# The last row of wo, loaded with its 2 KB blocks dealt in eights to the partitions

## The chip, the cores and the metric

The kernel runs on one core of one Trainium2 chip. A core has five engines with instruction queues of their own: TensorE (PE; its weight loads are shown apart as PEld), VectorE (DVE), ScalarE (ACT), GpSimd (POOL) and SyncE (SP). Sixteen DMA engines move data between HBM and the on-chip memory SBUF, which has 128 partitions; matmuls write to PSUM. Engines wait for one another through semaphores. The metric is the device time of one execution in microseconds (us).

## The reference: what is computed

One token of 1024 numbers goes through a layer norm, giving `xn`. Two branches use it, and both are added to the token:

```python
x = A_x
xn = _layernorm(x, axis=-1)
return x + _A_ref(xn, A_k_cache, A_v_cache, A_wq, A_wo) + _B_ref(xn, B_w1, B_b1, B_w2, B_b2)
```

Branch A is attention for one query position with 32 query heads and 4 key/value heads of size 128, over the last 4096 positions of the cache:

```python
q = (x @ wq).reshape(B, Sq, Hq, Dh).transpose(0, 2, 1, 3)
scores = jnp.einsum("bhqd,bhkd->bhqk", q, k) * (Dh ** -0.5)
p = _softmax(scores, axis=-1)
o = jnp.einsum("bhqk,bhkd->bhqd", p, v)
return o.transpose(0, 2, 1, 3).reshape(B, Sq, Hq * Dh) @ wo
```

Branch B is a small network: a second layer norm, `w1` (1024 x 3584) with bias `b1`, a gelu, `w2` (3584 x 1024) with bias `b2`. All inputs are bf16. The weights and the part of the caches that is used come to nearly 40 MB, and every byte of it is used once.

## The kernel before

**Loads.** All large loads are issued by SP, in this order: k (four loads, L73), wq (two, L90), w1 (two, L206), v (three, L212), w2 (two, L220) and wo (six, L228). They go into a ring of four tiles of 32 KB per partition (`ring_tile`), so a load is issued when the tile that it overwrites has been used. The DMA engines work through them in the order of issue. The small inputs (x, b1, b2) are loaded through ACT's queue (L75 to L81).

**wo.** `wo` is 4096 x 1024. `wo_v` (L222) views it as 128 partitions x 32 rows x 1024: partition p holds the rows 32p to 32p + 31 of the matrix. In what follows "row c of wo" is the slice `wo_v[:, c, :]`, that is one block of 1024 numbers (2 KB) for each of 128 partitions. Rows 0 to 15 come with one load into tile `wo0`. Rows 16 to 31 go into tile `wo1` in five loads, cut at 0, 8, 12, 14, 15 and 16 (L223), so that the last loads are small: rows 24 to 27, 28 and 29, 30, and 31.

**Compute up to the attention output.** The layer norms (L126 to L170) run on DVE, PE and POOL; POOL computes the power in L145 and L168 (`rstd`). DVE transposes k in blocks (L185), and ACT and DVE move the blocks into place (L199, L201). PE computes q (L237), the w1 products (L257), the scores (L275), and after the softmax the attention output `o_all` (L319). DVE makes `o_bf` of it (L322 to L326), which has a query head in each of 32 partitions and 128 numbers along the row.

**o8.** The product with wo needs o spread over 128 partitions in the same order as wo's rows: partition p, column c must hold number 32p + c of o. Number 32p + c belongs to head p // 4, at place 32 (p % 4) + c. Four matmuls (L328, L329) do that with the matrix `spread` (L111 to L114), made by POOL from a memset and a select: `spread[h, q, p]` is 1 where p = 4h + q and 0 elsewhere. DVE copies the result from PSUM to `o8` (L331).

**The last products.** `chunk_src` lists 28 rows of w2 ("h") and 32 rows of wo ("o"). The first 52 are the bulk (L336 to L339): two matmuls of 512 columns for each, added up in `accf`. The last eight (`TAIL`), rows 24 to 31 of wo, use four matmuls of 256 columns each (L351 to L354) into `acct`. While their loads arrive, DVE and ACT copy `accf` to `bulk` (L348, L350). At the end DVE adds `acct` and `bulk` (L356) and SP stores the result (L357).

Within an engine the order is that in which the instructions were emitted, except where the tile framework moved an instruction that has no dependence on its neighbours: on POOL the select for `spread` (L113) runs after the first `rstd` (L145), and the memset of `bulk` (L343) before it.

Of the kernel before, what the change touches and what calls it, by code (L numbers as in the profile page):

```python
# [9 lines left out]
BF16 = mybir.dt.bfloat16  # L10
# [6 lines left out]
def kernel(  # L17
# [14 lines left out]
    nc = tc.nc  # L32
    P = 128
# [5 lines left out]
    Hq = NQ // Dh  # L39
# [8 lines left out]
    CWO = NQ // P  # L48
# [6 lines left out]
    consts = ctx.enter_context(tc.tile_pool(name="consts", bufs=1))  # L55
# [8 lines left out]
    def ring_tile(name):  # L64
        return ring.tile([P, RING_ELEMS], BF16, tag="ring", name=name, align_bytes=256)
# [21 lines left out]
    for i in range(2):  # L87
        t = ring_tile(f"wq{i}")
        tv = t[:].rearrange("p (r n) -> p r n", r=4)
# [21 lines left out]
    spread = consts.tile([Hq, 4, P], BF16)  # L111
    nc.gpsimd.memset(spread[:], 0.0)
    nc.gpsimd.affine_select(out=spread[:], in_=spread[:], compare_op=ALU.not_equal, fill=1.0, base=0,  # L113
                            pattern=[[-1, 4], [1, P]], channel_multiplier=-4)  # L114

    gmask = consts.tile([Hq, Hkv], FP32)
    nc.gpsimd.memset(gmask[:], 1.0)
# [57 lines left out]
    for half in range(2):  # L175
        pr = 32 * half
        nc.tensor.matmul(accf[pr:pr + 1, :], lhsT=ones_bf[pr:pr + 2, 0:1], rhs=xb2[pr:pr + 2, :],
                         start=True, stop=False, tile_position=(pr, pr))
# [24 lines left out]
    for i in range(2):  # L203
        t = ring_tile(f"w1{i}")
        tv = t[:, :4 * Fd].rearrange("p (r n) -> p r n", r=4)
# [10 lines left out]
    for i in range(2):  # L216
        nr = CW2 // 2
        t = ring_tile(f"w2{i}")
        tv = t[:, :nr * D].rearrange("p (r n) -> p r n", r=nr)
        nc.sync.dma_start(out=tv, in_=w2_v[:, nr * i:nr * (i + 1), :])  # L220
        chunk_src += [("h", nr * i + r, tv[:, r, :]) for r in range(nr)]
    wo_v = A_wo.rearrange("(p c) n -> p c n", p=P)  # L222
    for i, cuts in enumerate([[0, 16], [0, 8, 12, 14, 15, 16]]):  # L223
        nr = CWO // 2
        t = ring_tile(f"wo{i}")
        tv = t[:].rearrange("p (r n) -> p r n", r=nr)
        for a, b in zip(cuts[:-1], cuts[1:]):
            nc.sync.dma_start(out=tv[:, a:b, :], in_=wo_v[:, nr * i + a:nr * i + b, :])  # L228
        chunk_src += [("o", nr * i + r, tv[:, r, :]) for r in range(nr)]


    for i, w3 in enumerate(wq_tiles):
        for r in range(4):
            c = 4 * i + r
            for j in range(NJQ):
                b, t = divmod(j, 4)
                nc.tensor.matmul(accq[32 * t:32 * t + 1, b, :], lhsT=xnT[:, c:c + 1], rhs=w3[:, r, j * 512:(j + 1) * 512],  # L237
                                 start=(c == 0), stop=(c == C - 1), tile_position=(0, 32 * t))
# [8 lines left out]
    for j in range(8):  # L247
        t, b = divmod(j, 2)
        nc.tensor.matmul(acch[32 * t:32 * t + 1, b, :NH], lhsT=ones_bf[0:1, 0:1], rhs=b1_row[:, j * NH:(j + 1) * NH],
                         start=True, stop=False, tile_position=(0, 32 * t))  # L250
    for i, w3 in enumerate(w1_tiles):
        for r in range(4):
            c = 4 * i + r
            for b in range(2):
                for t in range(4):
                    j = 2 * t + b
                    nc.tensor.matmul(acch[32 * t:32 * t + 1, b, :NH], lhsT=yT[:, c:c + 1], rhs=w3[:, r, j * NH:(j + 1) * NH],  # L257
                                     start=False, stop=(c == C - 1), tile_position=(0, 32 * t))
# [3 lines left out]
    for g in range(Hkv):  # L262
        b, th = divmod(g, 2)
# [6 lines left out]
    for a in range(WQ4 // 512):  # L270
        sp = ps_f.tile([P, 512], FP32, tag="pf", name="sp")
        for R in range(4):
            for g in range(Hkv):
                c0 = WQ4 * R + 512 * a
                nc.tensor.matmul(sp[32 * R:32 * R + 32, :], lhsT=qm[:, g, :], rhs=kT[:, g, c0:c0 + 512],  # L275
                                 start=(g == 0), stop=(g == Hkv - 1), tile_position=(0, 32 * R))
# [41 lines left out]
    for c in range(NCH):  # L318
        nc.tensor.matmul(o_all[:].rearrange("h g d -> h (g d)"), lhsT=eTb[:, 32 * c:32 * c + 32], rhs=v4[:, :, c, :],  # L319
                         start=(c == 0), stop=(c == NCH - 1))  # L320
# [4 lines left out]
    o_bf = consts.tile([Hq, Dh], BF16)  # L325
    nc.vector.tensor_copy(out=o_bf[:], in_=o_f[:])  # L326
    o8_ps = ps_f.tile([P, 32], FP32, tag="pf", name="o8_ps")
    for q in range(4):  # L328
        nc.tensor.matmul(o8_ps[:], lhsT=spread[:, q, :], rhs=o_bf[:, 32 * q:32 * q + 32], start=(q == 0), stop=(q == 3))  # L329
    o8 = consts.tile([P, 32], BF16)  # L330
    nc.vector.tensor_copy(out=o8[:], in_=o8_ps[:])  # L331

# [3 lines left out]
    for idx, (kind, c, wap) in enumerate(chunk_src[:n_bulk]):  # L336
        for half in range(2):
            nc.tensor.matmul(accf[32 * half:32 * half + 1, :], lhsT=vec[kind](c), rhs=wap[:, half * 512:(half + 1) * 512],  # L338
                             start=False, stop=(idx == n_bulk - 1), tile_position=(0, 32 * half))  # L339
# [11 lines left out]
    for idx, (kind, c, wap) in enumerate(chunk_src[n_bulk:]):  # L351
        for t in range(4):
            nc.tensor.matmul(acct[32 * t:32 * t + 1, :], lhsT=vec[kind](c), rhs=wap[:, t * 256:(t + 1) * 256],
                             start=(idx == 0), stop=(idx == TAIL - 1), tile_position=(0, 32 * t))  # L354
# [33 lines left out]
```

## Time and profile before

| what | value |
|---|---|
| time, median of 3 runs | 102.38 us (102.35 to 102.53) |
| profiled execution, first to last instruction (span) | 100.7 us; a time of its own beside the span is not listed |
| PE / DVE / ACT / POOL busy | 49% / 49% / 34% / 4% of the span |
| moved by DMA | 39.92 MB in 3031 packets, mean 396 GB/s |
| last load of wo | issued at 73.20 us, landed at 97.32 us |
| copy of o8 from PSUM (L331) | starts at 73.72 us, 0.19 us |
| PE waits for the first rows of wo (L338) | 6.09 us, until 87.59 us |
| L353, groups of the tail | 94.88, 96.10, 96.73 and 97.36 us |

Times in the profile count from the first instruction. A line such as `97.36 0.31 PE acct L353 x4` in the chain gives the start, the duration, the engine, the tile that is written, the line of the kernel and how many instructions were merged. "DMA wo<-in_A_wo_dram" in the chain is the time from the issue of a load to its landing, waiting behind other loads included. A table by stretches has one line for each stretch A:B, with its length, the busy time and number of instructions of PE, PEld, DVE, ACT and POOL, the granted clock of TensorE (1.00 is full), the mean busy share of the sixteen DMA engines, and the rate in GB/s. In the rows over 40 slices each digit is a share in tenths.

### The profile page before, as it was taken

What the parts mean: (1) busy time and instruction counts of PE and PEld (TensorE: products, weight loads), DVE (VectorE), ACT (ScalarE), POOL (GpSimd) and SP (SyncE); (2) the same over time, 40 slices, a digit from 0 to 9 for tenths busy, and PEclk for the clock granted to TensorE, in tenths of its full rate; (3) what the DMA queues carried; (4) which work ended last, traced back from release to release, by engine and by line L of the source; (5) the groups of instructions that cost most, each with busy time, mean ns of one, the idle gap of its engine ahead of it and who ended that gap; (6) DMA issues with size and microseconds to landing.
All of it is one profiled execution on the core that took longest, in us unless ns stands there. A gap on an engine that the chain in (4) does not pass through costs nothing.

```text
span 100.7 us, 962 instructions
## 1 busy us (share of the span) xinstructions
PE 49.1 (49%) x361; PEld 19.2 (19%) x361; DVE 49.4 (49%) x91; ACT 34.2 (34%) x37; POOL 4.5 (4%) x18
## 2 busy tenths in 40 slices
PE   0027200008500930482882935999389930299830
PEld 0012200003100300121531222334133410023310
DVE  4335499999999999997126115510630000000130
ACT  0500002999999999962001045400000000000110
POOL 7105300000000000000000000000000000000000
PEclk9999999999985579555555555569976997559995
DMA  3899999999999998999999998999999998999910
GB/s 52 346 434 436 482 443 482 443 430 417 417 417 391 456 444 376 459 444 382 391 423 430 436 511 387 467 428 433 433 410 413 456 456 384 423 420 408 369 33 1
DMA packets 3031, 39.92 MB, mean 396 GB/s; under 512 B 458, under 2 KB 466, under 8 KB 851
## 3 DMA queue, kind: packets, MB, share of 16 engines
q1 hardware_dynamic: 2872, 39.85, 93.3%
q8 instruction: 3, 0.05, 0.2%
q10 hardware_dynamic: 154, 0.01, 0.1%
q14 instruction: 2, 0.01, 0.0%
HBM read 39.86 MB, written 0.00 MB: 396 GB/s over the span
## 4 chain that ended last, share of the span: by engine, by line
DVE 37%; DMA 24%; PE 19%; issue 9%; POOL 3%; ACT 2%; SPq 2%; POOLq 1%; DVEq 0%; ACTq 0%
DMA wo<-in_A_wo_dram 24%; DVE kt_scr L185 17%; DVE kT L201 16%; PE o_all L319 10%; PE sp L275 4%; PE acch L257 3%; SPq L228 2%; ACT e L297 1%; DVE eTb L299 1%; DVE m_loc L283 1%; PE qT_ps L261 1%; DVE q_sb L240 1%; POOLq L383 1%; ACT sc L280 1%; POOL spread L113 1%
## 5 line engine op out<-in xcount | busy, mean ns | idle before, releaser
L199 ACT COPY kT<-kt_scr 32x1024 bf16<-32x1024 bf16 x26 | 27.1, 1042 | 12.9 <-DVE kt_scr L185 12.6
L185 DVE STREAM_TRANSPOSE kt_scr<-k_sb 128x4096 bf16<-128x4096 bf16 x4 | 17.4, 4412 | 0.0
L201 DVE COPY kT<-kt_scr 32x1024 bf16<-32x1024 bf16 x38 | 15.9, 419 | 0.5
L237 PE MATMUL accq<-wq,xnT 128*1 128x512 bf16 x64 | 7.1, 622 | 17.9 <-DMA wq<-in_A_wq_dram 17.9
L350 ACT COPY bulk<-accf 1x256 f32<-1x256 f32 x2 | 0.7, 361 | 31.7 <-DVE bulk L348 31.7
L348 DVE COPY bulk<-accf 1x256 f32<-1x256 f32 x2 | 0.8, 416 | 21.3 <-PE accf L338 20.8
L319 PE MATMUL o_all<-v_sb,eTb 128*32 128x512 bf16 x32 | 9.9, 485 | 1.0 <-DVE zcol L310 1.0
L338 PE MATMUL accf<-wo,o 128*1 128x512 bf16 x48 | 7.1, 465 | 6.1 <-DMA wo<-in_A_wo_dram 6.1
L257 PE MATMUL acch<-w,yT 128*1 128x448 bf16 x64 | 6.3, 574 | 5.6 <-DMA w<-in_B_w_dram 5.6
L338 PE MATMUL accf<-w,hT 128*1 128x512 bf16 x56 | 7.9, 452 | 0.0
L237 PEld LDWEIGHTS <-xnT 128*1 128x1 bf16 x64 | 2.1, 115 | 22.1 <-issue 22.1
L319 PEld LDWEIGHTS <-eTb 128*32 128x32 bf16 x32 | 3.7, 119 | 6.8 <-issue 3.8
L338 PEld LDWEIGHTS <-o 128*1 128x1 bf16 x48 | 2.4, 98 | 10.8 <-issue 8.9
L275 PE MATMUL sp<-kT,qm 128*32 128x512 bf16 x32 | 3.8, 629 | 0.3 <-DVE qm L266 0.3
L257 PEld LDWEIGHTS <-yT 128*1 128x1 bf16 x64 | 2.0, 116 | 9.4 <-issue 9.4
L131 PE MATMUL ln_tot<-st,ones_f 128*128 128x1 f32 x2 | 0.6, 362 | 6.4 <-DVE st L129 6.4
L338 PEld LDWEIGHTS <-hT 128*1 128x1 bf16 x56 | 2.7, 96 | 4.7 <-issue 2.3
L322 DVE TENSOR_TENSOR o_m<-o_all,grs 32x512 f32<-32x512 f32 x1 | 0.7, 679 | 5.6 <-PE o_all L319 5.6
L297 ACT ACTIVATE e<-sc,nmx 128x1024 bf16<-128x1024 f32 x1 | 1.1, 1147 | 5.7 <-DVE nmx L294 5.7
L314 DVE STREAM_TRANSPOSE hT<-h_sb 128x896 bf16<-128x896 bf16 x1 | 1.7, 1711 | 2.4 <-ACT h_sb L312 2.4
L261 PE MATMUL qT_ps<-ident,q_sb 128*128 128x128 bf16 x8 | 1.2, 308 | 2.3 <-DVE q_sb L240 2.3
L275 PEld LDWEIGHTS <-qm 128*32 128x32 bf16 x32 | 2.1, 133 | 1.4 <-issue 0.9
(84 smaller groups left out, 34.4 us busy)
## 6 DMA issues: line engine op xcount, KB each, us to landing
w<-in_B_w_dram SPq DMA_DIRECT2D x4, 3584.0 KB, 26.1
wq<-in_A_wq_dram SPq DMA_DIRECT2D x2, 4096.0 KB, 21.6
k_sb<-in_A_k_cache_dram SPq DMA_DIRECT2D x4, 1024.0 KB, 7.1
wo<-in_A_wo_dram SPq DMA_DIRECT2D x1, 4096.0 KB, 29.4
v_sb<-in_A_v_cache_dram SPq DMA_DIRECT2D x1, 2048.0 KB
v_sb<-in_A_v_cache_dram SPq DMA_DIRECT2D x2, 1024.0 KB, 23.4
wo<-in_A_wo_dram SPq DMA_DIRECT2D x1, 2048.0 KB
wo<-in_A_wo_dram SPq DMA_DIRECT2D x1, 1024.0 KB, 23.1
```

The costliest lines, as they stand in the source:

```text
L185: nc.vector.transpose(out=scr[:, g, :], in_=k2[:, g, :])
L199: nc.scalar.copy(out=dst, in_=src)
L201: nc.vector.tensor_copy(out=dst, in_=src)
L228: nc.sync.dma_start(out=tv[:, a:b, :], in_=wo_v[:, nr * i + a:nr * i + b, :])
L237: nc.tensor.matmul(accq[32 * t:32 * t + 1, b, :], lhsT=xnT[:, c:c + 1], rhs=w3[:, r, j * 512:(j + 1) * 512], start=(c == 0), stop=(c == C ...
L257: nc.tensor.matmul(acch[32 * t:32 * t + 1, b, :NH], lhsT=yT[:, c:c + 1], rhs=w3[:, r, j * NH:(j + 1) * NH], start=False, stop=(c == C - 1) ...
L261: nc.tensor.transpose(qT_ps[:, b * 4 + hh, :], q_sb[:, b, hh * Dh:(hh + 1) * Dh], ident[:])
L275: nc.tensor.matmul(sp[32 * R:32 * R + 32, :], lhsT=qm[:, g, :], rhs=kT[:, g, c0:c0 + 512], start=(g == 0), stop=(g == Hkv - 1), tile_posit ...
L297: nc.scalar.activation(out=e128[:], in_=sc[:], func=ACT.Exp, bias=nmx[:], scale=scale, accum_out=l_loc[:])
L314: nc.vector.transpose(out=hT[:], in_=h_sb[:].rearrange("p (d c) -> p c d", c=CW2))
L319: nc.tensor.matmul(o_all[:].rearrange("h g d -> h (g d)"), lhsT=eTb[:, 32 * c:32 * c + 32], rhs=v4[:, :, c, :], start=(c == 0), stop=(c == ...
L338: nc.tensor.matmul(accf[32 * half:32 * half + 1, :], lhsT=vec[kind](c), rhs=wap[:, half * 512:(half + 1) * 512], start=False, stop=(idx == ...
```

## The change

Row 31 of wo is loaded in another arrangement. Its 128 blocks of 2 KB are the matrix rows 32p' + 31 for p' = 0 to 127. Before, block p' goes to partition p'. After, p' is written as 8b + a with a from 0 to 7 and b from 0 to 15, and the source is walked with a outermost: block 8b + a goes to partition 16a + b. The access pattern of the source then has the sizes 8, 16 and 1024, and that of the destination 128 and 1024. The row is still one load, issued last of all on SP's queue, of the same 256 KB.

Column 31 of `o8` has to stand in the same order. A second matrix `spread_p` is made from `spread` by a copy on POOL that permutes its 128 columns in the same way (32 partitions x 512, bf16). The four matmuls of L329 now make the columns 0 to 30, and four more, of one column each, make column 31 with `spread_p`. The copy to `o8` and everything behind it stay as they were.

```diff
@@ -112,6 +112,8 @@
     nc.gpsimd.memset(spread[:], 0.0)
     nc.gpsimd.affine_select(out=spread[:], in_=spread[:], compare_op=ALU.not_equal, fill=1.0, base=0,
                             pattern=[[-1, 4], [1, P]], channel_multiplier=-4)
+    spread_p = consts.tile([Hq, 4, P], BF16)
+    nc.gpsimd.tensor_copy(out=spread_p[:].rearrange("h q (a b) -> h q a b", a=8), in_=spread[:].rearrange("h q (b a) -> h q a b", a=8))
 
@@ -220,12 +222,14 @@
     wo_v = A_wo.rearrange("(p c) n -> p c n", p=P)
-    for i, cuts in enumerate([[0, 16], [0, 8, 12, 14, 15, 16]]):
+    for i, cuts in enumerate([[0, 16], [0, 8, 12, 14, 15]]):
         nr = CWO // 2
         t = ring_tile(f"wo{i}")
         tv = t[:].rearrange("p (r n) -> p r n", r=nr)
         for a, b in zip(cuts[:-1], cuts[1:]):
             nc.sync.dma_start(out=tv[:, a:b, :], in_=wo_v[:, nr * i + a:nr * i + b, :])
+        if i == 1:
+            nc.sync.dma_start(out=tv[:, nr - 1, :], in_=wo_v[:, CWO - 1, :].rearrange("(b a) n -> a b n", a=8))
         chunk_src += [("o", nr * i + r, tv[:, r, :]) for r in range(nr)]
@@ -326,7 +330,9 @@
     o8_ps = ps_f.tile([P, 32], FP32, tag="pf", name="o8_ps")
     for q in range(4):
-        nc.tensor.matmul(o8_ps[:], lhsT=spread[:, q, :], rhs=o_bf[:, 32 * q:32 * q + 32], start=(q == 0), stop=(q == 3))
+        nc.tensor.matmul(o8_ps[:, 0:31], lhsT=spread[:, q, :], rhs=o_bf[:, 32 * q:32 * q + 31], start=(q == 0), stop=(q == 3))
+    for q in range(4):
+        nc.tensor.matmul(o8_ps[:, 31:32], lhsT=spread_p[:, q, :], rhs=o_bf[:, 32 * q + 31:32 * q + 32], start=(q == 0), stop=(q == 3))
     o8 = consts.tile([P, 32], BF16)
```

## The prediction

> **What bounds the kernel now.** I read the busy table and the queue table first, then the chain that ended last, then the busy time of short stretches at the end.
>
> From the page: the queue table, and the slices of DMA share and rate.
>
> ```profile
> DMA  3899999999999998999999998999999998999910
> GB/s 52 346 434 436 482 443 482 443 430 417 417 417 391 456 444 376 459 444 382 391 423 430 436 511 387 467 428 433 433 410 413 456 456 384 423 420 408 369 33 1
> ...
> q1 hardware_dynamic: 2872, 39.85, 93.3%
> q8 instruction: 3, 0.05, 0.2%
> ```
>
> No compute engine is over half busy (PE and DVE 49%), while the sixteen DMA engines are busy from slice 2 to slice 38 and SP's queue fills 93.3% of their time. The kernel is one stream of 39.85 MB, and its time is that stream, its start (first data at 1.8 us) and what follows its last packet. The three instruction packets (q8, 16 KB each) will matter.
>
> The end of the chain, asked for from 70 us:
>
> ```profile
> 73.20 24.12 DMA wo<-in_A_wo_dram
> 97.32 0.04 issue
> 97.36 0.31 PE acct L353 x4
> 97.67 0.03 issue
> 97.70 0.02 DVEq L356
> 97.72 0.04 issue
> 97.76 0.42 DVE res L356
> ```
>
> The last row of wo lands at 97.32 us. Four matmuls, one add and the store follow, and the span ends at 100.7: whatever moves that landing moves the end by as much. The chain's 24 us of DMA are queueing behind earlier loads.
>
> How the DMA engines run dry, by stretches (after the busy times of PE, PEld, DVE, ACT and POOL come the granted clock, the DMA share and GB/s):
>
> ```profile
> 94.60:95.20 0.60, 0.38 (x14) 0.29 (x16) 0.41 (x1) 0.00 (x0) 0.00 (x0) 1.00 1.05 410
> 95.20:95.50 0.30, 0.29 (x12) 0.08 (x1) 0.00 (x0) 0.30 (x1) 0.00 (x0) 1.00 0.66 253
> 95.50:95.80 0.30, 0.00 (x0) 0.00 (x0) 0.20 (x1) 0.06 (x1) 0.00 (x0) 1.00 0.31 116
> 96.00:96.80 0.80, 0.46 (x12) 0.25 (x12) 0.01 (x1) 0.36 (x1) 0.00 (x0) 1.00 0.13 49
> 96.80:97.40 0.60, 0.25 (x8) 0.06 (x7) 0.00 (x0) 0.00 (x0) 0.00 (x0) 1.00 0.02 7
> ```
>
> From 96.0 to 96.8 the share is 0.13, two engines of sixteen (2/16 = 0.125): fourteen have finished and two are late. This is the resource that the change touches. The trace's packet records, one line per packet, give the rest. A 2 KB packet starts every 0.080 us on one engine, so an engine's eight packets of the last row take 0.64 us. The closing packets of that row come at 95.18 to 95.80 us on thirteen engines, at 95.98 on one, and at 96.78 and 96.99 on the late two; the landing is seen 0.33 us after the last (97.32). The late ones were not slow by nature: a 16 KB instruction packet at 45.89 us halted one for 0.92 us and stretched its next packet from 1.06 to 1.56 us, and a second did the same to the other at 67.55 us. Each lost some 1.4 us and never caught up. The third, at 95.89 us, met an engine that was already done.
>
> **The change part by part.** The sum goes against this execution's span of 100.7 us; no separate time of it is shown, and the median of three runs, 102.38 us, lies 1.68 us above the span. I add differences to the median.
>
> *The last row's DMA.* The source now has 8 as its outer size, with 16 rows of wo under each, so eight engines carry 16 packets each and eight carry none. A carrier ends 8 x 0.080 = 0.64 us later; an engine left out is free after row 30, 0.64 us earlier. Everything depends on where the two late engines fall:
> - the later one carries: 96.99 + 0.64 + 0.33 = 97.96 us instead of 97.32, so +0.64 us;
> - only the other late one carries: 96.78 + 0.64 + 0.33 = 97.75, so +0.43 us;
> - neither carries: the carriers end between 95.80 + 0.64 = 96.44 and 95.98 + 0.64 = 96.62, landing at 96.77 to 96.95. Row 30 still needs the late engines, whose packets of it close by 96.34 and land by 96.69; its matmuls start at 96.73, and four more behind them cost 0.11 us (a group of eight took 0.39, of four 0.28). So the last four start at 96.84 to 96.99 instead of 97.36: 0.37 to 0.52 us won.
>
> Which eight carry is not shown before the change. For a blind draw neither late engine carries with 8/16 x 7/15 = 0.23. Two facts help. The load of b1 (one row) and those of x and b2 (two rows each) lie on two engines, by the gaps that their packets leave, and neither of the two is late; if loads of few pieces always use the same first engines, those two are carriers and the chance is 8x7/(14x13) = 0.31. Those two were also third and fifth of the sixteen to end their first packet of k (2.90 and 2.92 us), the late ones tenth to twelfth (3.18 and 3.20), which would fit an order by number. I go to 0.40.
>
> A rule of the Trainium skill weighs in here ("DMA: Bandwidth & Descriptors", "Why a DMA increments its semaphore by 16 and not by 1"): such a DMA takes the largest number of engines up to 16 that divides the outer sizes of both sides, and the lowest-numbered of them. By it the carriers are engines 0 to 7. The same page ("Latency and other measured facts") notes that engines 7 and 15 tend to be the slow ones, without a sure cause; were those the late two, exactly one would carry and the sum would be +0.43 or +0.64 us. The trace ties the lateness to instruction packets instead, and names no engine. The page's "Rules for kernel authors" speak against the change as well: use all 16.
>
> *Port and memory side.* Each engine now fills sixteen neighbouring partitions from rows of wo eight blocks apart. No row has that shape. Below: nothing, as 2 KB packets keep 0.080 us. Above: the worst stretch of a packet in the trace outside instruction traffic, 1.31 for 1.06 us, a quarter, on 1.28 us: 0.3 us. I take 0.05, as the packets keep their size; I leave it out of the first two cases, where the late engine runs alone.
>
> *Issue on SP.* One DMA for another, behind the five of L228. It is issued at 73.20 and its data move at 94.5 or later, so a longer issue (the plain ones took 0.33, the strided ones 0.43) is hidden by some 20 us of queued loads. Without that cover it would cost perhaps 0.1 us.
>
> *spread_p on POOL.* One copy of 32x512 bf16. The nearest rows are the select (L113, 0.63 us) and the memset (L112, 0.51) of that size; a strided read could double it to 1.3. POOL is idle for 1.27 us before rstd (L168). If the copy overruns, rstd, yT and the transposes L185 behind them on DVE move by as much, at most some 0.8 us. What is late next is SP's load of v and w2 into the freed tiles; the second w1 load was issued at 30.1 us and moved at 40.4, w2 was issued at 45.0 and moved at 58.7. That queue hides it: 0. It cannot gain, since nothing is removed there.
>
> *Four more matmuls and weight loads at L329.* The four old ones took 0.25 us; 31 columns instead of 32 change nothing, four of one column add 0.1 to 0.25 us. Behind them on PE stand the L338 matmuls of hT, and on DVE the copy o8 (L331) waits too. PE later idles 6.09 us for wo before 87.6, so nothing reaches the end. Without that idle time, up to 0.25 us.
>
> *PE's instruction stream.* Eight instructions longer, so the third instruction packet may come up to 0.4 us earlier (eight at the bulk's rate, four matmuls in 0.43 us). Its engine ends by 95.80 now; as a carrier it would be busy until 96.44 and the packet, even at 95.89, would stop it for 0.92 us: up to 97.36, where the late engines end at 96.99 now. That would eat the gain of the third case.
>
> **The rivals.**
> - *Forecast: a late engine carries.* For it: two of sixteen are late and eight carry. +0.64 us if it is the later one (103.02), +0.43 if the other (102.81).
> - *Neither late engine carries* (the other side): for it, the order of first packets; against, the draw. It decides from the point at which both late engines lie among the idle eight. 0.37 to 0.52 us less 0.05: 101.9 to 102.1, centre 101.95.
> - *Neither carries, but a carrier meets the third instruction packet*: 97.36 + 0.33 = 97.69 against 97.32 is +0.37 for the last of the ordinary engines, and for the first of them (95.18 + 0.64 + 0.92 + 0.33 = 97.07) it is -0.25; about 102.4.
> - *The DMA still spreads over sixteen*, the split being read off the 128 partitions: the same bytes per engine, 102.38.
>
> **How the numbers follow.** Later engine carries 0.34, only the other 0.20, neither 0.34, third packet 0.06, still sixteen 0.06. The likeliest is the first, 103.0, with its own range 102.85 to 103.15. Both signs hold much of the chance, so the wide range goes from the third case's gain (101.85) to the first case's loss with a little for landing (103.15). 0.2%, 0.2 us, is about what can be told from no change: faster 0.34, same 0.12, slower 0.54.
>
> **What would show it.** In the short stretches: a DMA share near 0.5 (eight engines) from about 95.2 to 95.8, then for the forecast 0.06 to 0.13 up to about 97.6, with the L353 group of the last row starting near 98.0. A share that reaches zero by 96.7 and a last group near 96.9 shows the opposite case; an unchanged 0.13 up to 96.8 shows sixteen engines. The copy on POOL should end before rstd L168 starts, and PE's wait for wo before 87.6 should stay near 6 us. The forecast is wrong if the instruction packets strike engines that don't carry, or move in the longer program.

## The result, and the profile after

| | before | after |
|---|---|---|
| time, median of 15 runs each | 102.35 us (102.15 to 102.53) | 102.83 us (102.49 to 103.35) |
| ratio | 1 | 1.0053, 95% interval 1.0036 to 1.0069 |
| span of the profiled execution | 100.7 us | 100.9 us |
| landing of row 30 of wo | 96.69 us | 97.34 us |
| landing of row 31, the last | 97.32 us | 97.51 us |

The change costs 0.48 us. The forecast was 103.0 us, slower, because a late DMA engine would carry sixteen packets. The time fits; the profile shows another cause in the execution that was traced. That execution took 102.57 us, near the low end of its fifteen times, and its span is 0.2 us longer than that of before: the trace accounts for 0.2 of the 0.48 us. Lines of after are six further down than those of before (L353 is now L359, L356 is L362).

The chain that ended last, of after, its last pieces:

```profile
72.82 24.52 DMA wo<-in_A_wo_dram
97.34 0.04 issue
97.38 0.48 PE acct L359 x8
97.86 0.03 issue
97.89 0.02 DVEq L362
```

The landing at 97.34 us in this chain is that of row 30: its load is the one that SP issued at 72.82 us (L230). Row 31 has a line of its own now, L232, issued at 73.29 us. The trace's landing events, one for each engine that has finished its part of a load, put its last at 97.51 us. The eight matmuls are those of both rows. PE from 97.66 us on, of after, has those of row 31 alone:

```profile
97.55 0.28 PE L359 MATMUL acct<-wo,o 128*1 128x256 bf16 x4
```

Row 31 lands 0.19 us later than before (97.51 for 97.32), its matmuls start 0.19 us later (97.55 for 97.36) and so does DVE's add (97.95 for 97.76), which is the 0.2 us between the spans. Row 30, whose load was not changed, lands 0.65 us later and is now almost as late as row 31.

The short stretches at the end, of after (busy times of PE, PEld, DVE, ACT, POOL, then the granted clock, the DMA share and GB/s):

```profile
94.60:95.20 0.60, 0.45 (x18) 0.30 (x17) 0.41 (x1) 0.00 (x0) 0.00 (x0) 1.00 0.88 341
95.20:95.50 0.30, 0.27 (x12) 0.07 (x1) 0.00 (x0) 0.24 (x1) 0.00 (x0) 1.00 0.70 225
95.50:95.80 0.30, 0.00 (x0) 0.00 (x0) 0.15 (x1) 0.12 (x1) 0.00 (x0) 1.00 0.71 184
96.00:96.80 0.80, 0.02 (x4) 0.02 (x6) 0.07 (x1) 0.36 (x1) 0.00 (x0) 1.00 0.38 136
96.80:97.40 0.60, 0.39 (x12) 0.18 (x12) 0.00 (x0) 0.00 (x0) 0.00 (x0) 1.00 0.03 10
```

Fewer engines work than before from 94.6 to 95.2 (0.88 against 1.05), more than before from 95.5 on (0.71 against 0.31), and from 96.0 to 96.8 the mean share is 0.38, six engines of sixteen, where it was two. Then it stops: the row's last packet closes at 97.07 us. An engine that was late and carried sixteen packets would have gone on to about 97.6. So this is neither the forecast's picture (0.06 to 0.13 up to 97.6) nor that of the case without a late carrier (zero by 96.7).

PE's last groups, of before:

```profile
94.88 0.61 PE L353 MATMUL acct<-wo,o 128*1 128x256 bf16 x16 [0.22 <-DMA wo<-in_A_wo_dram]
96.10 0.39 PE L353 MATMUL acct<-wo,o 128*1 128x256 bf16 x8 [0.61 <-DMA wo<-in_A_wo_dram]
96.73 0.28 PE L353 MATMUL acct<-wo,o 128*1 128x256 bf16 x4 [0.24 <-DMA wo<-in_A_wo_dram]
97.36 0.28 PE L353 MATMUL acct<-wo,o 128*1 128x256 bf16 x4 [0.35 <-DMA wo<-in_A_wo_dram]
```

and of after:

```profile
94.86 0.61 PE L359 MATMUL acct<-wo,o 128*1 128x256 bf16 x16
96.78 0.39 PE L359 MATMUL acct<-wo,o 128*1 128x256 bf16 x8 [1.31 <-DMA wo<-in_A_wo_dram]
97.38 0.45 PE L359 MATMUL acct<-wo,o 128*1 128x256 bf16 x8 [0.21 <-DMA wo<-in_A_wo_dram]
```

This is the telling view. The second group of each is rows 28 and 29, and their load was not touched: the same bytes, on the same sixteen engines. They come 0.68 us later (96.78 for 96.10). The group of eight at 97.38 holds row 30's four matmuls and, from 97.55 on, row 31's. Something holds up engines that still write old rows while the new one is under way.

The packet records and landing events narrow it down. Row 30 and row 31 are 256 packets of 2 KB; before, the longest takes 0.084 us. After, 60 of the 256 take more than 0.090 us and the longest 0.201, and 6 of the 128 packets of 4 KB (rows 28 and 29) take more than 0.170, up to 0.353. The wait for the landing grows as well: from the end of the last packet of rows 28 and 29 to their landing it is 0.36 us before (95.70 to 96.06) and 0.61 after (96.13 to 96.74). So 0.43 of the 0.68 us lie in the packets and 0.25 behind them.

### The profile page after: what moved, and what is told of

The parts are those of the page before. It is cut to its first block, busy times and chain, and to the rows that moved or that the text cites. A ratio compares the mean times of both kernels' runs of the same rounds, so it can differ in the third digit from the quotient of the medians.

```text
span 100.9 us, 971 instructions
## 1 busy us (share of the span) xinstructions
PE 49.2 (49%) x365; PEld 19.3 (19%) x365; DVE 49.4 (49%) x91; ACT 34.2 (34%) x37; POOL 5.5 (5%) x19
## 3 DMA queue, kind: packets, MB, share of 16 engines
q1 hardware_dynamic: 2864, 39.85, 93.4%
## 4 chain that ended last, share of the span: by engine, by line
DVE 37%; DMA 24%; PE 19%; issue 8%; POOL 4%; ACT 2%; SPq 1%; POOLq 1%; DVEq 0%; ACTq 0%
DMA wo<-in_A_wo_dram 24%; DVE kt_scr L187 17%; DVE kT L203 16%; PE o_all L323 10%; PE sp L279 4%; PE acch L261 3%; ACT e L301 1%; DVE eTb L303 1%; DVE m_loc L287 1%; PE qT_ps L265 1%; SPq L230 1%; POOL spread_p L116 1%; DVE q_sb L244 1%; POOLq L389 1%; ACT sc L284 1%
## 5 line engine op out<-in xcount | busy, mean ns | idle before, releaser
L356 ACT COPY bulk<-accf 1x256 f32<-1x256 f32 x2 | 0.7, 362 | 31.7 <-DVE bulk L354 31.7
```

## Experiments

The expectations weigh these explanations, some by a letter. *A late engine carries*, also *L*, is the forecast. *M*: packets that are written at the same time hold each other up. *S*: rows of wo read eight blocks apart are slower to read. *V*: the instruction packets strike other DMA engines in each execution, so that which engine is late is no property of the program; *F* is its opposite, always the same engines. For the packets, the table that all of this section draws on (from the packet records and landing events; "late" are engines that close rows 16 to 23 after 91.6 us, the others do so at 90.1 to 91.3; "lag" is the time from the end of the last packet of rows 28 and 29 to their landing):

| kernel | 2 KB packets over 0.090 us (of 256), longest | lag | late engines | last packet closes | row 30, row 31 land | time against before |
|---|---|---|---|---|---|---|
| before | 0, 0.084 | 0.36 | 2 | 96.99 | 96.69, 97.32 | 1 |
| after | 60, 0.201 | 0.61 | 2 | 97.07 | 97.34, 97.51 | 1.0053 |
| the same once more | 54, 0.193 | 0.79 | 2 | 96.88 | 97.36, 97.31 | one time, 102.53 us |
| plain load, new matmuls | 0 | 0.38 | 2 | 96.97 | 96.68, 97.30 | 0.9992 |
| four loads of 32, first trace | 1, 0.125 | 0.54 | 2 | 97.59 | 97.31, 97.94 | 1.0044 |
| four loads of 32, three more | 17, 16, 11; 0.184 | 0.94, 0.94, 0.81 | 2 | 96.97, 96.87, 96.82 | 97.43, 97.41; 97.39, 97.26; 97.24, 97.27 | one time each |
| one load over sixteen | 38, 0.187 | 0.57 | 2 | 97.28 | 97.13, 97.65 | 1.0048 |
| two loads of 64 | 58, 0.206 | 0.69 | 2 | 97.24 | 97.45, 97.68 | 1.0063 |
| row 31 in partitions 0 to 63 | 0, 0.084 | 0.34 | 2 | 96.69 | 96.80, 97.04 | 1.0024 |
| plain load, fewer matmuls | 4, 0.232 | 0.32 | 0 | 96.97 | 95.82, 97.40 | 1.0024 |
| plain load, fewest matmuls | 0, 0.084 | 0.32 | 0 | 96.06 | 95.77, 96.42 | 0.9926 |
| changed load, fewest matmuls | 2, 0.101 | 0.33 | 0 | 96.61 | 95.75, 96.98 | 1.0001 |

The lag falls into two groups: 0.32 to 0.38 us in six traces, 0.54 to 0.94 in eight.

### The compute side alone

The load of row 31 is plain again; the copy on POOL and the four more matmuls stay.

```diff
-            nc.sync.dma_start(out=tv[:, nr - 1, :], in_=wo_v[:, CWO - 1, :].rearrange("(b a) n -> a b n", a=8))
+            nc.sync.dma_start(out=tv[:, nr - 1:nr, :], in_=wo_v[:, CWO - 1:CWO, :])
...
-        nc.tensor.matmul(o8_ps[:, 31:32], lhsT=spread_p[:, q, :], ...
+        nc.tensor.matmul(o8_ps[:, 31:32], lhsT=spread[:, q, :], ...
```

> The new copy on POOL and the four more matmuls stay; row 31 is loaded as before, its blocks in their old places, and column 31 of o8 is made with the old matrix. All theories that put the loss on the load: 102.35 us, within 0.2 of before, with thirteen engines done by 95.8 us and two late ones up to about 97.0. If the added instructions cost the time (or move the instruction packets to worse places): 102.6 to 102.9.

Measured: 102.38 us against 102.41, 0.9992 [0.9979, 1.0005]. Within that interval the compute side costs nothing, and the loss belongs to the load.

### Other splits of the same row

Four loads of 32 blocks each, every one of outer size 8:

```diff
-            nc.sync.dma_start(out=tv[:, nr - 1, :], in_=wo_v[:, CWO - 1, :].rearrange("(b a) n -> a b n", a=8))
+            for g0 in range(0, P, 32):
+                nc.sync.dma_start(out=tv[g0:g0 + 32, nr - 1, :],
+                                  in_=wo_v[g0:g0 + 32, CWO - 1, :].rearrange("(b a) n -> a b n", a=8))
```

In this and the other splits the columns of `spread_p` are put in the matching order (not shown).

> Row 31 still goes to eight engines by blocks dealt in eights, but in four loads of 32 partitions, so that each engine fills four neighbouring partitions in each load and no two of the eight work in the same group of four; the source step between an engine's blocks stays eight blocks. Theory M (meeting in SBUF: in the changed kernel two engines at a time walk through the same partitions' write path, and disturb the late engines too, which do not carry): packets keep 0.08 us, the last group of matmuls starts at 96.9 to 97.1, time 101.9 to 102.1. Theory L (a late engine carries sixteen packets, as forecast): 102.8 to 103.0, last packets near 97.4 to 97.6. Theory S (the source step slows the reads): as the changed kernel, 102.7 to 102.9, packets of 0.1 to 0.2 us.

One load with an outer size of 16 (`a=16` in the load and in the copy of `spread_p`):

> Row 31 in one load dealt in sixteens, so that all sixteen engines carry eight packets as before, but each into eight neighbouring partitions and from blocks sixteen apart. Theory M: engines meet in pairs, and more of them, so packets of the last row stretch to 0.1 to 0.2 us on all, the late ones included: 102.6 to 103.2. Theory L: no engine carries more than before, so 102.35. Theory S: stretched packets as well, 102.6 to 103.0.

Two loads of 64 blocks (`range(0, P, 64)`):

> Row 31 on eight engines in two loads of 64 partitions, each engine filling eight neighbouring partitions, so that engines meet in pairs again (a with a + 4) but in half of SBUF at a time. Theory M: between the changed kernel and the four loads, 102.2 to 102.8, with stretched packets. Theory L: 102.8 to 103.0. Theory S: 102.7 to 102.9.

Measured: four loads 102.95 us, 1.0044 [1.0025, 1.0064]; one load over sixteen 102.90, 1.0048 [1.0031, 1.0065]; two loads 103.02, 1.0063 [1.0042, 1.0084]. Every arrangement loses about as much as the change. The trace of the four loads shows the forecast's case as it was drawn. Its chain, from 80 us:

```profile
87.61 10.33 DMA wo<-in_A_wo_dram
97.94 0.04 issue
97.98 0.31 PE acct L362 x4
```

and its stretches:

```profile
95.80:96.40 0.60, 0.00 (x1) 0.00 (x0) 0.22 (x1) 0.35 (x1) 0.00 (x0) 1.00 0.64 222
96.40:97.00 0.60, 0.39 (x8) 0.18 (x8) 0.20 (x1) 0.36 (x1) 0.00 (x0) 1.00 0.17 65
97.00:97.60 0.60, 0.25 (x4) 0.09 (x3) 0.00 (x0) 0.00 (x0) 0.00 (x0) 1.00 0.06 24
```

In the last stretch 0.06 is one engine of sixteen. It closes its packets of the four loads at 96.62, 96.94, 97.27 and 97.59, and the row lands at 97.94; the forecast had 97.96. Only one packet of 256 is stretched here, yet row 30 lands 0.62 us later than before (97.31 for 96.69) and the lag is 0.54, so the rows before are held up here too. So the forecast's mechanism exists, but not in the trace of after. Either the four loads go to other engines than the one load does, or the late engines were others in that execution.

The load of outer size 16 runs on all sixteen engines (2872 packets on SP's queue as before; after has eight closing packets fewer, 2864). So "eight engines instead of sixteen" is not the only cost: each engine has its eight packets again, and it is as slow.

### The same kernel in three more executions

The kernel with four loads, unchanged, in three more executions with one trace each:

> The kernel with four loads of 32 partitions once more, for another trace. In its first trace an engine that had lost time to an instruction packet carried sixteen packets of row 31 (its four loads closed at 96.62, 96.94, 97.27 and 97.59 us), while in the profiled execution of the changed kernel neither late engine carried. Theory V (the instruction packets strike other engines from one execution to the next): the number of late engines that carry varies between 0, 1 and 2 over these traces, and the end with it: last packet near 97.0 us with none, 97.4 to 97.8 with one or two. Theory F (always the same engines): the first trace again each time, one late engine carrying, last packet near 97.6.

> A third trace of the four loads of 32 partitions. Theory V: a late engine carries in some of the traces and not in others, last packet near 97.0 or near 97.4 to 97.8. Theory F: last packet near 97.6 each time.

> A fourth trace of the four loads of 32 partitions, with the same expectations as the third.

Measured: 103.00, 102.75 and 102.80 us, spans 101.3, 101.0 and 101.1 (before beside them 102.26). In none does a late engine carry: the last packets close at 96.97, 96.87 and 96.82, against 97.59 in the first trace of the same kernel, and 11 to 17 packets are stretched instead of 1. The chain of the first of them:

```profile
97.43 0.04 issue
97.48 0.62 PE acct L362 x8
```

Rows 30 and 31 are taken together, as in after. So whether a late engine carries is not settled by the program, which speaks for V. These three ran on another chip than the first, so the chip might decide instead of the execution: no chip shows both cases in its traces. On the first chip the ten times of this kernel fall into two groups, four at 102.49 to 102.64 and six at 102.90 to 103.29, as two cases would give. But the time alone doesn't tell the cases apart: 103.00 us was measured without a late carrier, 0.74 above before on that chip. The change itself, once more:

> The changed kernel once more, for a second trace. If the instruction packets always strike engines that don't carry: last packets again within 97.0 to 97.2 us, with the group of rows 28 and 29 late at 96.7 or 96.8. If they strike other engines in other executions: possibly a late engine among the carriers, last packets at 97.4 to 97.8 and a time above 103.1.

Measured: 102.53 us, span 100.8, and again no late engine carries (last packet 96.88). The times of after have a gap, though: nine of fifteen lie at 102.49 to 102.87 and six at 103.11 to 103.35. That six of them are executions with a late carrier would fit (0.5 us between the middles of the two groups); none of them has a trace, and the 103.00 us above came without one, so this stays open.

### Fewer instruction packets

A kernel whose TensorE program is 248 instructions long instead of 708, so that fewer instruction packets are fetched; the loads are those of before. Most of the products are left out (of wq, k, v, w1, w2 and the first half of wo).

```diff
+            if 0 < c < C - 1:
+                continue
...
+        if (kind == "h" and c % 14) or (kind == "o" and c < 16 and c % 8):
+            continue
...
```

> The kernel before with all its loads, but most matmuls left out: six of eight rows of wq, seven of eight of w1, two of four heads' scores, thirty of thirty-two steps of the value product, most rows of w2 and of the first half of wo. TensorE's program falls from 708 to 248 instructions. If the 16 KB packets carry TensorE's instructions and they alone make the two engines late: none comes before the last loads, no engine is held for 0.9 us, all sixteen end the last row within about 0.8 us of one another, it lands near 96.3 instead of 97.3 us, and the time falls by 0.8 to 1.1 us to about 101.4. If the late engines are slow for another reason: the last row still lands near 97.3 and the time stays within 0.3 of 102.4.

Measured: 102.52 us, 1.0024 [1.0006, 1.0042]. One instruction packet is left of three. No engine closes rows 16 to 23 later than 91.16, so the lateness of the two engines did come from the other two. But the one that is left comes at 95.00, meets an engine in its last packets, and that engine closes at 96.97 while all others are done by 96.15. The run could not show the gain. Still fewer products (left in are one row of wq, w1 and w2 each, the scores of two of four heads, two of 32 steps of the product with v, and rows 0 and 23 of the bulk of wo), 196 instructions on PE:

> The kernel before with all its loads and still fewer matmuls than in the run with 248 instructions (one row of eight of wq and w1, two of four heads' scores, two of thirty-two steps of the value product, one row of w2, two of the bulk's rows of wo; 196 instructions). The one instruction packet that came at 95.0 us there should come after the stream or not at all. If instruction packets alone make engines late: last packet near 95.7 to 96.0 us, last group of matmuls at 96.0 to 96.4, time 101.1 to 101.6. If not: 102.2 to 102.5.

Measured: 101.63 us, 0.9926 [0.9903, 0.9949]: 0.75 us less. Here the last instruction packet hits an engine where it does no harm. The queue table and the last stretches:

```profile
q8 instruction: 1, 0.02, 0.1%
```

```profile
95.20:95.80 0.60, 0.53 (x8) 0.16 (x8) 0.00 (x0) 0.00 (x0) 0.00 (x0) 1.00 0.38 137
95.80:96.40 0.60, 0.38 (x4) 0.09 (x4) 0.00 (x0) 0.00 (x0) 0.00 (x0) 1.00 0.03 10
```

The engines are done by 96.06 us, 0.93 earlier than before, and the last row lands at 96.42. PE was not the bound (it is 15% busy here, 49% before), and all sixteen engines now close rows 16 to 23 at 90.1 to 91.1 us, as fourteen did before (90.2 to 91.0), so in this stream leaving out products changed the two late engines alone. Neither kernel gives the right result; they show a cause and are no way to gain. The Trainium skill ("Runtime: NRT & Kernel Launch", "Instruction fetch mechanics") calls the cost of crossing to the next 16 KB block of instructions mostly hidden. These runs disagree for this kernel, which is bound by DMA: the price falls on the DMA engine that fetches (0.92 us of standstill and a stretched packet), and so on the end of the stream.

Now the change in that kernel without late engines: the same products left out, the load over eight engines and the copy and matmuls with it.

> The same matmuls left out of the changed kernel (204 instructions), so that row 31 in one load of eight engines meets no engine that an instruction packet made late. Against the run with 196 instructions on the same chip: by the sixteen packets alone +0.5 to 0.65 us, with the meeting of engines in neighbouring partitions +0.7 to 1.2 us, packets of row 31 stretched to 0.1 to 0.2 us. If all of the loss came from late engines that carry: not above +0.65 and no stretched packets.

Measured: 102.33 us, against the last kernel 102.33 - 101.63 = +0.70 us; landing 96.98 for 96.42, +0.56. Its stretches:

```profile
95.20:95.80 0.60, 0.45 (x11) 0.13 (x3) 0.00 (x0) 0.00 (x0) 0.00 (x0) 1.00 0.52 201
95.80:96.40 0.60, 0.38 (x4) 0.08 (x4) 0.00 (x0) 0.00 (x0) 0.00 (x0) 1.00 0.27 102
96.40:97.00 0.60, 0.00 (x0) 0.00 (x0) 0.00 (x0) 0.00 (x0) 0.00 (x0) 1.00 0.02 7
```

From 95.2 on half of the engines work, as the change says, then fewer, and nothing is stretched (2 of 256). With no engine late, moving eight packets from one half of the engines to the other costs about what eight packets cost.

### Row 31 in the lower half of the partitions

The row goes to a tile of 64 partitions in two halves, by four loads of outer size 8; its product becomes two of half height.

```diff
+            row31 = consts.tile([64, 2, D], BF16)
+            for g0 in range(0, P, 32):
+                nc.sync.dma_start(out=row31[g0 % 64:g0 % 64 + 32, g0 // 64, :],
+                                  in_=wo_v[g0:g0 + 32, CWO - 1, :].rearrange("(b a) n -> a b n", a=8))
...
```

> Row 31 still goes to eight engines dealt in eights in four loads of 32 partitions, but all of it into partitions 0 to 63, two blocks to a partition, with two half-height products at the end in place of one (four more small matmuls before, four more last ones, about 0.1 us). If what undoes the gain of the four loads is that carriers writing partitions 64 to 127 meet the two late engines, which still write rows 28 to 30 there: no packet stretches, the carriers end by 96.0 to 96.6 us, the last group of matmuls starts at 96.8 to 97.0, and the time is 101.9 to 102.2, the first version under the kernel before; executions in which a late engine carries come out at 102.8 to 103.2. If it isn't that meeting: 102.5 to 103.2 with stretched packets, like the four loads.

Measured: 102.57 us against 102.38, 1.0024 [1.0004, 1.0045]. PE's groups:

```profile
96.19 0.39 PE L368 MATMUL acct<-wo,o 128*1 128x256 bf16 x8 [0.60 <-DMA wo<-in_A_wo_dram]
96.84 0.28 PE L368 MATMUL acct<-wo,o 128*1 128x256 bf16 x4 [0.26 <-DMA wo<-in_A_wo_dram]
97.05 0.39 PE L368 MATMUL acct<-row,o 64*1 64x256 bf16 x8
```

No packet is stretched, the lag is 0.34 us, rows 28 and 29 are back at 96.19 and row 31 (landed at 97.04) is there before row 30's products end: the picture that the prediction had drawn for its case without a late carrier (last group at 96.84 to 96.99). The result of DVE starts at 97.56 instead of 97.76. Even so the span is 100.66 against 100.70 us, since the time behind the store is longer by nearly as much (1.35 for 1.17 us from its last packet to the end). That goes with the number of loads and not with the partitions: it is 1.34 to 1.35 us in all five traces with four loads for row 31, 1.21 with two, and 1.16 to 1.17 in the eight traces with one. So all kernels with four loads pay some 0.18 us that has nothing to do with how the row arrives. The time of 101.9 to 102.2 us was not reached. Nine of its twelve times lie at 102.31 to 102.60, level with before, three, without a trace, at 102.98 to 103.33.

## Why the prediction was right, and where not

- **The time** was right: 102.83 measured, 103.0 forecast, within its range, and slower was the likeliest sign. The range, 101.85 to 103.15, held both signs. In the executions that were traced the way to it was another, so the nearness is in part luck.
- **"The later one carries" failed for the traced executions.** In two traces of the change out of two neither late engine is among the eight. That is the case to which the prediction gave 0.34 and 101.95 us. The step behind it, one placement of late engines and carriers for the program, doesn't hold either, by the kernel with four loads: a late carrier in one trace of four, the one from another chip. The prediction named this as what would make it wrong, but gave it no term. The draw has to be made for each execution, or each chip, and a median can then be a mixture.
- **"Port and memory side" was the term that was mis-sized.** It was taken at 0.05 us, bounded by 0.3, and charged to the row's own packets alone. In after the carriers close at 97.07 where the case without a late carrier had 96.44 to 96.62: 0.45 to 0.63 us. Its landing came 0.44 us behind that, where the prediction took 0.33, so at 97.51 instead of 96.77 to 96.95. That eats the whole of the 0.37 to 0.52 us to be won. It fell on other rows too: 28 and 29 came 0.68 us later, and row 30 landed at 97.34, where the prediction had 96.69. The trace adds up to +0.19 us. So the forecast's +0.64 and the measured +0.48 are not the same sum.
- **Sixteen packets at 0.080 us, 0.64 us for eight more: right** where nothing stretches them: +0.70 us in time and +0.56 us in landing between the two kernels with fewest matmuls, and 97.94 for the forecast 97.96 where a late engine carried.
- **Late engines come from instruction packets: right**, shown by taking the packets away (none late, and 0.75 us less once the remaining one did no harm).
- **The load runs on eight engines: right.** The trace of after has eight landing events for it. It agrees with the number of engines in the rule that the prediction cited of the Trainium skill ("DMA: Bandwidth & Descriptors", "Why a DMA increments its semaphore by 16 and not by 1"). Which eight they are, no run here shows.
- **The third instruction packet comes up to 0.4 us earlier: it did not**, and without effect. It is at 95.92 us, for 95.89, and met no carrier.
- **What was put at nothing is nothing.** In after's trace, the copy on POOL takes 1.07 us, between the bounds of 0.63 and 1.3, and `rstd` behind it starts at 11.85 us; the four more matmuls take 0.23 us in front of an idle time of 5.9 us; the issue on SP takes 0.77 us instead of 0.43, more than the 0.1 that the prediction had for it, hidden all the same. The profile lines of after:

```profile
10.28 1.07 POOL L116 COPY spread_p<-spread 32x512 bf16<-32x512 bf16 x1
11.85 0.56 POOL L170 TENSOR_TENSOR rstd<-ve,mhalf 128x1 f32<-128x1 f32 x1 [0.36 <-DVE ve L168]
73.29 0.77 SPq L232 DMA_DIRECT2D wo<-in_A_wo_dram  x1
73.62 0.23 PE L335 MATMUL o_ps<-o_bf,spread_p 32*128 32x1 bf16 x4
```

**What stays open.** What the stretched packets share. The runs bound it, by one trace each where nothing else is said: it needs late engines (60 packets and a lag of 0.61 us with, 2 and 0.33 without, for the same load); it is absent when the row stays in partitions 0 to 63 (0 packets and 0.34, with late engines, against 1 to 17 and 0.54 to 0.94 in four traces of the same four loads over all partitions); it is not the step of eight blocks in the source, which the kernels with 0 and 2 stretched packets have too, so S falls; and it is not the number of carriers (38 packets with sixteen). That the carriers simply collide with each other, M in its first form, falls with the kernel of fewest matmuls, in which eight carry side by side undisturbed. That carriers which write the upper partitions slow those that still write the rows before is what is left, and it is argued, not shown: the records name no partition, and the kernel with the row in partitions 0 to 63 also writes to another tile, which no run tells apart. Open too are the untraced slower times of after, and why four loads lengthen the time behind the store. No version that computes everything was faster than before.

## What to carry to other kernels

When a kernel is one DMA stream, look at the last packet of each DMA engine, and ask why the last engine is last: here it had stood still for an instruction fetch, and taking those fetches away, at the price of most of the products, was worth 0.75 us, while every new split of the last load lost in a kernel that computes everything. Moving work from some engines to others helps only if the same engines are late in every execution, so look at several traces before relying on one, and charge the full n packets to the engines that get more. Rows whose loads you did not touch show whether the new load gets in the way of the others; compare when they land, not only how long their packets take. And check which load a landing in the chain belongs to, by the time at which it was issued: here it was not the last one.

## What the runs showed of the hardware

- A load that was not changed landed 0.68 us later when another load's blocks were spread differently over the engines and partitions; a 2 KB packet went from 0.084 us to as much as 0.201, and the time from the last packet to the landing from 0.36 us to 0.61 (0.94 with four loads).
- Whether a DMA engine made late by an instruction packet is one that carries the last load differs between traces of one program (one of four, that one from another chip).
- A load that walks its source in eights took SP 0.77 us to issue, against 0.43 for a plain strided one.
- The time from the store's last packet to the end of the span was 1.16 to 1.17 us in the eight traces with one load for row 31, 1.21 with two loads, and 1.34 to 1.35 in the five with four.
